# A gated linear attention and MLP-mixer kernel: another hand-fixed issue order and another buffer numbering

## The chip, the cores and the metric

One core of a Trainium2 chip runs the kernel. The metric is the device time of one execution in microseconds, taken as the median of several executions of the same program. The engines of the core work side by side, each through its own queue in order: TensorE (PE, with its weight loads shown apart as PEld), VectorE (DVE), ScalarE (ACT), GpSimd (POOL) and SyncE (SP), whose queue here only issues transfers.

## The reference

The input is q, k, v and alpha of shape (4, 8, 768, 48) and four mixer weights; the output is (4, 768, 384) in float32.

```python
# attention: a recurrence over t, for each of 4 batches and 8 heads
state = alpha[:, :, t, :, None] * state + np.einsum('bhd,bhe->bhde', k[:, :, t], v[:, :, t])
y[:, :, t] = np.einsum('bhd,bhde->bhe', q[:, :, t], state)
# x = y with heads side by side, (4, 768, 384); then the mixer
h = np.maximum(xt @ w_tok1, 0.0) @ w_tok2        # xt is x with tokens last
u = x + h.transpose(0, 2, 1)
out = u + np.maximum(u @ w_ch1, 0.0) @ w_ch2
```

## The kernel before, in words

The recurrence is computed in blocks. Each batch of 768 tokens is cut into 3 blocks of 256, so there are 12 blocks, numbered n = 0 to 11; a block has two halves of 128 tokens, and each SBUF row holds two neighbouring tokens. For block n the kernel loads alpha, k, q and v (`ld_at`, `ld_kt`, `ld_qt`, `ld_vt`, L584, 384 KB each). It takes logarithms on ACT (`ln`, L631, L634, L637), sums them along the tokens on PE (`cum`, `cumw`, L643) and takes exponentials of the sums and of their negatives on ACT (`E`, L676 and L683; `IE`, L679 and L687). k is multiplied by `IE` and q by `E` (`kk`, `qq`, L700, on DVE or POOL). Both products are transposed, on PE for blocks 0 to 5 (`trk`, `trq`, L712, with the evictions `evk`, `evq`, L745 on ACT or L746 on DVE) and by DMA for blocks 6 to 11 (`dk`, `dq`, L725, with one more copy `pq`). `G0_n` and `G1_n` are the products of keys and queries on PE, `mask0_n` and `mask1_n` their masked evictions on DVE (L770). `K` makes the new state, which DVE and POOL add to the old one (`s`, L837; `sa`, L841; `sm`, L844). `ia`, `ib` and `y0`, `y1` give a half's output on PE, and `x0`, `x1` take it out of PSUM.

The mixer of batch b follows. `t1_b_m_kc` (L878) and `t2_b_i` (L883) are the token products with the eviction `ht` between them, and `u_b_i` (L887, DVE) adds x. u is transposed on PE for batch 0 (`up`, L894, with the evictions `ut`) and by DMA for batches 1 to 3 (`ux_b_0` and `ux_b_1`, L729, one for each half of the tokens). `c1_b_mc_half` (L902) is a group of three 384-wide matmuls; `rt_b_mc_half` evicts it with a maximum (L873 on ACT, L875 on DVE). `c2_b_i_q` (L907) is a group of three matmuls over three of the twelve `rt`; `o_b_i` (L911, DVE) adds u and `st_b_i` (L624) stores the result. The weights come in 16 loads of 384 KB (`ldw_wt1`, `ldw_wt2`, `ldw_wc1`, `ldw_wc2`, L600 to L607), each followed by a cast (`cw`). The first six of the twelve column blocks of `wc1` need its pieces 0, 1 and 2, the other six its pieces 3, 4 and 5.

Nothing is scheduled while the program is built. `build` (L121) makes all operations with their inputs and outputs. The table `ORDER` names them one after the other, each with a letter for its engine (t PE, s ACT, v DVE, g POOL, y SP), and they are emitted in exactly that order, so it sets every queue. `BUFS` gives each value its buffer number: 19 buffers for loads (`in`), 8 PSUM banks, 20 for `rt`, 3 for `o`, 2 to 4 for most others. A value waits until the last reader of its buffer is done. `fillers` (L130) offers filler operations named `f8_x`, which multiply zeros into a free PSUM bank ahead of the operation x; the number counts units of one 512-wide matmul, and every three units become one float32 matmul of 64 rows (`fill`, L645). The order lists only some of them. `shared` (L732) makes every SBUF-to-SBUF operation on DVE wait for the last such operation on POOL, and the other way round.

Of the kernel before, what the change touches and what calls it, by code (L numbers as in the profile page):

```python
# [421 lines left out]
rt_0_9_0v rt_0_11_1v E4s c1_0_7_0t c1_0_10_1t c1_0_7_1t ldw_wc10y r14s cw_wc10s rt_0_10_1v trq3t evk3s rt_0_7_0v
ldw_wc12y ld_vt3y cw_wc12g c1_0_2_0t c1_0_0_1t ka3g rt_0_7_1s c1_0_8_1t rt_0_10_0v vb3v vs1_3g vs0_3g rt_0_0_1v
rt_0_2_0v evq3s ld_at5y ld_qt4y c1_0_1_1t rt_0_8_1v c1_0_3_0t kc3s K3t P5g c1_0_4_1t rt_0_3_0s rt_0_1_1s q0r4g G0_3t
ld_kt4y qq4g s0_3v ln15s G1_3t sa1_3v c1_0_2_1t rt_0_2_1s mask0_3v lnP5s c1_0_1_0t c1_0_5_1t rt_0_5_1s rt_0_1_0s r15s
mask1_3v ldw_wc21y cw_wc21s k0a4g ldw_wc20y c1_0_6_1t rt_0_6_1v c1_0_4_0t kk4v ldw_wc22y c1_0_5_0t c1_0_0_0t cw_wc22s
rt_0_4_0v rt_0_0_0v cw_wc20g rt_0_4_1s c1_0_6_0t rt_0_6_0v c1_0_3_1t trq4t rt_0_3_1v cum5t trk4t ld_kt5y k0a5g
ldw_wc23y rt_0_5_0s c2_0_3_0t c2_0_5_0t evq4s kb4s evk4v ld_qt5y G1_4t mask1_4v G0_4t ld_vt4y c2_0_0_0t IE5s c2_0_0_1t
ka4g cw_wc23s c2_0_3_1t kc4s sm1_3g E5s mask0_4v ib3t y1_3t ldw_wc24y cw_wc24s c2_0_5_1t vb4g vs1_4s x1_3s ia4t
ldw_wc25y vs0_4g cw_wc25s ld_at6y y0_3t kk5v c2_0_3_2t y0_4t q0r5v trk5t evk5s qq5v K4t c2_0_0_2t sa0_4v c2_0_0_3t P6v  # L430
x0_3s ld_at7y sm0_4g o_0_0v trq5t x0_4s sa1_4v P7g evq5s lnP6s c2_0_5_2t c2_0_5_3t ld_vt5y vb5g c2_0_4_0t c2_0_4_1t
ld_kt7y kc5g G1_5t G0_5t lnP7s o_0_5v ib4t y1_4t vs1_5s mask1_5v t1_1_1_0t t1_1_1_1t sm1_4g x1_4s c2_0_4_2t c2_0_3_3t
vs0_5s ld_at8y t1_1_1_2t st_0_5s K5t mask0_5v sa0_5v sm0_5v cum6t t1_1_0_0t ld_kt6y k0a6g t1_1_0_1t ld_qt6y c2_0_2_0t
# [532 lines left out]
```

## Time and profile before

| what | us |
|---|---|
| median of three executions | 163.17 (162.33, 163.17, 164.11) |
| span of the profiled execution, first to last instruction | 160.5 |
| what lies around the span, if the profiled execution took the median | 2.7 |
| first instruction to the first `c1` group of batch 0 | 31.76 |
| that point to the end of the last matmul | 125.66 |
| end of the last matmul to the end of the span | 3.08 |

The profiled execution has no time of its own beside its span. The times of the table's lower rows are read off the timeline of PE. A row of a timeline gives the start, the length, the engine, the line and operation, the tiles, the count of merged instructions, and in brackets the engine's idle time ahead of it and what ended that. A matmul's row lasts longer than the distance to the next matmul's start, because matmuls are pipelined: distances between starts say how fast PE works.

### The profile page before, as it was taken

Reading aid. Unit: us, or ns where it says so; the run is one execution under the profiler, and the core shown is the slowest. Engines: PE = TensorE matmul, PEld = TensorE weight load, DVE = VectorE, ACT = ScalarE, POOL = GpSimd, SP = SyncE. Lnnn points to the kernel's source line nnn. Section 1 sums busy time; section 2 is a strip of 40 time slices with the busy share of each in tenths; the row PEclk is TensorE's granted clock in tenths of the full one; section 3 lists DMA queues with packets and bytes.
Section 4 is the critical chain, followed back from the end, with each engine's and each line's share of the span. In section 5 each row is a group of like instructions: output and inputs, shape, how many; then the busy total and the mean of one; then the engine's idle time right before and its main releaser. Section 6 shows DMA issues by size and latency. Waiting matters only on the chain.

```text
span 160.5 us, 3971 instructions
## 1 busy us (share of the span) xinstructions
PE 154.6 (96%) x1563; PEld 97.1 (60%) x1563; DVE 114.9 (72%) x206; ACT 97.8 (61%) x179; POOL 80.8 (50%) x94
## 2 busy tenths in 40 slices
PE   7999989999999999999999999999999999999992
PEld 2545565766667676666667666566567665665661
DVE  6099994979889787989969758795886762464222
ACT  3789999998899955897563583269832203343000
POOL 5205897695973649389778852699523000000000
PEclk9999999999999999999999999999999999999999
DMA  4999999999999999999989999989701235111133
GB/s 122 320 324 317 317 374 311 339 333 306 316 347 324 275 278 272 210 228 319 241 202 298 239 315 204 217 196 134 196 21 62 87 79 169 49 49 53 49 129 116
DMA packets 76130, 35.05 MB, mean 218 GB/s; under 512 B 70352, under 2 KB 74320, under 8 KB 76112
## 3 DMA queue, kind: packets, MB, share of 16 engines
q1 hardware_dynamic: 73808, 31.76, 74.1%
q10 hardware_dynamic: 2304, 3.05, 5.3%
q8 instruction: 12, 0.20, 0.5%
q14 instruction: 6, 0.05, 0.1%
HBM read 25.17 MB, written 4.72 MB: 186 GB/s over the span
## 4 chain that ended last, share of the span: by engine, by line
PE 61%; DMA 12%; DVE 6%; ACT 6%; SPq 6%; POOL 4%; issue 3%; DVEq 0%; POOLq 0%
PE ps L907 22%; PE ps L902 21%; PE ps L643 11%; DMA in<-in_v_dram 6%; SPq L584 6%; DMA out_dram<-o 4%; PE ps L878 3%; PE ps L883 2%; DMA ut<-u 2%; DVE pkk L700 2%; DVE gtm L770 1%; PE ps L712 1%; DVE rt L875 1%; POOL vb L746 1%; POOL pkq L700 1%
## 5 line engine op out<-in xcount | busy, mean ns | idle before, releaser
L907 PE MATMUL ps<-wc,rt 128*128 128x384 bf16 (+1 forms) x300 | 52.4, 319 | 0.0
L902 PE MATMUL ps<-ut,wc 128*128 128x384 bf16 x288 | 50.3, 326 | 0.1
L902 PEld LDWEIGHTS <-wc 128*128 128x128 bf16 x288 | 27.1, 98 | 17.9 <-DMA ut<-u 0.6
L907 PEld LDWEIGHTS <-rt 128*128 128x128 bf16 x300 | 27.8, 98 | 16.0
L873 ACT ACTIVATE rt<-ps 128x384 bf16<-128x384 f32 x47 | 21.4, 492 | 23.6 <-PE ps L902 23.3
L875 DVE TENSOR_SCALAR rt<-ps 128x384 bf16<-128x384 f32 x49 | 25.6, 551 | 9.1 <-PE ps L902 8.9
L770 DVE TENSOR_TENSOR gtm<-ps,mk 128x1024 bf16<-128x1024 f32 x24 | 28.5, 1218 | 3.1 <-PE ps L643 2.8
L911 DVE TENSOR_TENSOR o<-ps,u 128x384 f32<-128x384 f32 (+1 forms) x25 | 13.2, 536 | 12.6 <-PE ps L907 10.1
L700 POOL TENSOR_TENSOR pkk<-in,IE 128x768 bf16<-128x768 f32 x8 | 14.5, 1817 | 3.3 <-DVE ss L844 2.3
L745 ACT CAST x<-ps 128x384 bf16<-128x384 f32 x20 | 9.2, 479 | 11.1 <-PE ps L643 9.5
L887 DVE TENSOR_TENSOR u<-ps,x 128x384 bf16<-128x384 f32 x24 | 12.0, 550 | 3.1 <-PE ps L883 2.5
L746 POOL CAST vb<-in 64x384 bf16<-64x384 f32 (+1 forms) x14 | 8.3, 594 | 10.4 <-DMA in<-in_v_dram 4.7
L692 POOL TENSOR_TENSOR in<-in,in 128x384 f32<-128x384 f32 x8 | 8.0, 1000 | 10.5 <-DVE u L887 3.8
L643 PE MATMUL ps<-rt 128*128 128x512 bf16 (+1 forms) x29 | 12.1, 515 | 1.1 <-DVE rt L541 1.1
L745 ACT CAST vb<-in 64x384 bf16<-64x384 f32 (+1 forms) x18 | 11.4, 634 | 0.8 <-DMA in<-in_v_dram 0.3
L700 POOL TENSOR_TENSOR pkq<-in,E 128x768 bf16<-128x768 f32 x6 | 10.9, 1818 | 0.6 <-DMA tpk<-pkq 0.3
L878 PE MATMUL ps<-x,wt 128*128 128x384 bf16 x48 | 11.0, 325 | 0.0
L844 POOL TENSOR_TENSOR ss<-tmp,E 128x384 bf16<-128x384 f32 x10 | 8.3, 833 | 4.2 <-DVE in L628 3.9
L841 DVE TENSOR_TENSOR tmp<-ps,ss 128x384 f32<-128x384 f32 x16 | 8.8, 552 | 1.8 <-PE ps L643 0.6
L883 PE MATMUL ps<-ht,wt 128*128 128x384 bf16 x48 | 9.1, 326 | 0.0
L643 PE MATMUL ps<-vb,gtm 128*128 128x48 bf16 x192 | 8.2, 183 | 0.2 <-DVE gtm L770 0.2
L643 PE MATMUL ps<-tpq,tpk 48*64 48x128 bf16 (+1 forms) x288 | 7.9, 218 | 0.4 <-POOL tpq L746 0.3
(94 smaller groups left out, 207.6 us busy)
## 6 DMA issues: line engine op xcount, KB each, us to landing
in<-in_alpha_dram SPq DMA_DIRECT2D x12, 384.0 KB, 5.1
in<-in_v_dram SPq DMA_DIRECT2D x12, 384.0 KB, 5.6
in<-in_k_dram SPq DMA_DIRECT2D x12, 384.0 KB, 5.2
in<-in_q_dram SPq DMA_DIRECT2D x12, 384.0 KB, 5.5
in<-in_moe_w_ch_dram SPq DMA_DIRECT2D x12, 384.0 KB, 5.9
out_dram<-o ACTq DMA_DIRECT2D x15, 192.0 KB, 1.8
in<-in_moe_w_tok_dram SPq DMA_DIRECT2D x4, 384.0 KB, 6.0
out_dram<-o SPq DMA_DIRECT2D x8, 192.0 KB, 2.2
```

Of the source, the lines that this page charges most:

```text
L643: return self.pe.matmul(out, lhsT=lhsT, rhs=rhs, start=start, stop=stop, skip_group_check=True)
L700: self.shared(self.eng[e].tensor_tensor(self.t(dst)[:, :, h0:h1, 0:D], self.t(src)[:, h0:h1].rearrange("p h s d -> p s h d"), bass.AP(tens ...
L745: return self.act.copy(d, s)
L770: self.nc.vector.tensor_tensor(self.t(gtm)[:, hf, :, :], self.pair(gp).rearrange("p a (j t) -> p (a j) t", t=128), bass.AP(tensor=m.tensor ...
L873: self.act.activation(d, s, AF.Relu)
L875: self.nc.vector.tensor_scalar_max(d, s, 0.0)
L878: self.pe.matmul(self.bank(bank)[:, 0:HD], lhsT=self.wt1[:, kc, m * 128 : m * 128 + 128], rhs=self.t(x), start=(kc == 0), stop=(kc == NS - 1))
L883: self.pe.matmul(self.bank(bank)[:, 0:HD], lhsT=self.wt2[:, kc, i * 128 : i * 128 + 128], rhs=self.t(hts[kc]), start=(kc == 0), stop=(kc = ...
L887: self.nc.vector.tensor_tensor(self.t(u)[:, i % 3], self.bank(bank)[:, 0:HD], self.t(x), ALU.add)
L902: self.pe.matmul(self.bank(bank)[:, 0:HD], lhsT=self.wc1[:, kc, mc * 128 : mc * 128 + 128], rhs=self.t(ut)[:, 3 * half : 3 * half + 3, kc, ...
L907: self.pe.matmul(self.bank(bank)[:, 0 : cz - ca], lhsT=self.t(rts[mc][0])[:, i * 128 : i * 128 + 128], rhs=self.wc2[:, mc, ca:cz], start=( ...
L911: self.nc.vector.tensor_tensor(self.t(o)[:, ca:cz], self.bank(bank)[:, 0 : cz - ca], self.t(u)[:, i % 3, ca:cz], ALU.add)
```

## The change

The two tables are replaced; no other line differs. The names in the new `ORDER` are the same operations but for the fillers, and what each operation computes is the same. Three things differ: the order on every engine, the engine of 147 operations that may run on more than one, and the buffer numbers. Of the diff, whose rows are tables of names, these lines show the kind:

```diff
-ld_at1y ld_at0y ln1s ln0s f8_cumw1t f1_cumw1t cumw1t IE1s cumw0t IE0s ld_vt0y E0s vb0g vs0_0g vs1_0v ld_kt0y kk0v
+ld_kt1y ld_at0y ln0s f12_cumw0t f2_cumw0t cumw0t ld_at1y ln1s cumw1t ld_qt0y E0s qq0v f2_trq0t trq0t ld_kt0y IE0s kk0v
...
-11 8 0 1 0 0 2 1 2 1 0 12 0 0 0 4 2 1 1 0 4 3 8 1 4 0 0 5 1 6 6 9 0 1 7 0 12 0 0 7 2 0 1 0 0 1 0 1 2 4 1 7 1 3 2 2 1 6
+6 0 0 7 0 0 0 1 1 2 1 1 2 0 7 4 3 0 5 1 7 0 6 1 0 0 0 0 4 8 1 0 4 0 7 2 2 0 5 7 0 1 0 0 10 9 1 6 6 1 4 7 6 0 0 1 1 0 1
```

The fillers before are `f8_cumw1 f1_cumw1 f8_trk0 f1_trk0 f1_trq0 f1_trk1 f2_G0_0 f4_cumw2 f3_y1_0 f2_ia1 f1_G0_2 f1_t1_0_1_5 f3_t2_0_0`, 36 units of which 9 stand ahead of the first `cumw`. Now they are `f12_cumw0 f2_cumw0 f2_trq0 f1_cumw2 f4_trq1 f1_trq1 f4_G1_1 f2_trk2`, 28 units of which 14 stand ahead of the first `cumw`.

The first place is SP's queue at the start of the program, where the loads of blocks 0 to 2 stand. Before, its first nine loads are these (`in_` is a load buffer; the tensor behind the arrow tells alpha, k, q or v):

```order
L584 DMA in_75<-in_alpha_dram 128x8x96
L584 DMA in_72<-in_alpha_dram 128x8x96
L584 DMA in_76<-in_v_dram 128x8x96
L584 DMA in_64<-in_k_dram 128x8x96
L584 DMA in_65<-in_q_dram 128x8x96
L584 DMA in_72<-in_k_dram 128x8x96
L584 DMA in_69<-in_v_dram 128x8x96
L584 DMA in_73<-in_alpha_dram 128x8x96
L584 DMA in_76<-in_q_dram 128x8x96
```

Now they are these:

```order
L584 DMA in_70<-in_k_dram 128x8x96
L584 DMA in_64<-in_alpha_dram 128x8x96
L584 DMA in_65<-in_alpha_dram 128x8x96
L584 DMA in_66<-in_q_dram 128x8x96
L584 DMA in_67<-in_k_dram 128x8x96
L584 DMA in_71<-in_v_dram 128x8x96
L584 DMA in_68<-in_alpha_dram 128x8x96
L584 DMA in_72<-in_v_dram 128x8x96
L584 DMA in_65<-in_q_dram 128x8x96
```

The load of block 1's k now comes first, and q and k of block 0 come ahead of its v. Behind these, the six pieces of `wc1` are loads 20, 21, 22, 24, 25 and 26 before, with a load of q as number 23, and loads 20 to 25 now.

The second place is DVE's queue in the middle of the `c1` groups of batch 0, around the masks of block 3 (`gtm`). Tile numbers are kept: `rt` are evictions of `c1` groups, `vb` a cast of v, `ss` and `tmp` the state, `pkq` the scaled q, `tpq` an eviction of transposed q. Before:

```order
L875 TENSOR_SCALAR rt_3_136<-ps_63 128x384
L875 TENSOR_SCALAR rt_8_141<-ps_63 128x384
L746 CAST vb_0_98<-in_2_66 128x768
L875 TENSOR_SCALAR rt_9_142<-ps_63 128x384
L875 TENSOR_SCALAR rt_6_139<-ps_63 128x384
L875 TENSOR_SCALAR rt_1_134<-ps_63 128x384
L837 TENSOR_TENSOR ss_1_112<-ps_63,E_1_88 128x384
L841 TENSOR_TENSOR tmp_1_110<-ps_63,ss_1_112 128x384
L770 TENSOR_TENSOR gtm_1_108<-ps_63,mk_166 128x1024 x2
```

Now:

```order
L696 TENSOR_TENSOR in_3_67<-in_3_67,lf_0_85 128x8x48
L700 TENSOR_TENSOR pkq_1_93<-in_3_67,E_0_87 128x16x48
L875 TENSOR_SCALAR rt_5_138<-ps_63 128x384
L875 TENSOR_SCALAR rt_0_133<-ps_63 128x384
L746 COPY tpq_1_106<-ps_63 128x2x512
L875 TENSOR_SCALAR rt_8_141<-ps_63 128x384
L875 TENSOR_SCALAR rt_6_139<-ps_63 128x384
L875 TENSOR_SCALAR rt_9_142<-ps_63 128x384
L770 TENSOR_TENSOR gtm_1_108<-ps_63,mk_166 128x1024 x2
L875 TENSOR_SCALAR rt_3_136<-ps_63 128x384
L837 TENSOR_TENSOR ss_1_112<-ps_63,E_0_87 128x384
L841 TENSOR_TENSOR tmp_0_109<-ps_63,ss_1_112 128x384
```

The scaling of block 3's q (`in_3` and `pkq_1`) and the eviction of its transpose (`tpq_1`), which were POOL's and ACT's before, now stand in DVE's queue, and the cast `vb_0` left it. From the first `rt` up to the eviction of `c1_0_10_1`, DVE now has 14 `rt`, two masks, two evictions of transposed q, one of transposed k, the two scalings of q and two of the state.

The third place is SP's queue ahead of the DMA transposes of u for batch 2 (`ut` from `u`). Before:

```order
L584 DMA in_82<-in_k_dram 128x8x96
L584 DMA in_73<-in_q_dram 128x8x96
L584 DMA in_69<-in_v_dram 128x8x96
L584 DMA in_64<-in_k_dram 128x8x96
L624 DMA out_dram<-o_155 128x384
L624 DMA out_dram<-o_153 128x384
L729 DMA_TRANSPOSE ut_131<-u_128 128x9x128
L729 DMA_TRANSPOSE ut_131<-u_127 128x9x128
L725 DMA_TRANSPOSE tpk_103<-pkq_93 128x8x128
L725 DMA_TRANSPOSE tpk_102<-pkk_96 128x8x128
```

Now:

```order
L725 DMA_TRANSPOSE tpk_104<-pkk_96 128x8x128
L725 DMA_TRANSPOSE tpk_103<-pkq_92 128x8x128
L584 DMA in_79<-in_v_dram 128x8x96
L584 DMA in_81<-in_k_dram 128x8x96
L584 DMA in_64<-in_q_dram 128x8x96
L584 DMA in_73<-in_q_dram 128x8x96
L584 DMA in_76<-in_k_dram 128x8x96
L725 DMA_TRANSPOSE tpk_101<-pkq_93 128x8x128
L725 DMA_TRANSPOSE tpk_102<-pkk_94 128x8x128
L729 DMA_TRANSPOSE ut_131<-u_127 128x9x128
L729 DMA_TRANSPOSE ut_131<-u_128 128x9x128
```

The two stores (`out_dram`) ahead of the transposes of u left this queue, the transposes of block 9 (`tpk` from `pkq` and `pkk`) moved ahead of them, and five loads instead of nine stand behind the transposes of block 8. Around the same stage for batch 1, PE now has two `c2` groups, `cum8`, `K6` and five `c1` groups between the end of `t2_1_5` and the first `c1` group of the second half, `c1_1_7_1`.

Of the 25 stores, 15 moved between the queues of ACT and SP. The last three before were issued by ACT (`st_3_4`), ACT (`st_3_1`) and SP (`st_3_0h0`, a half), and now by SP (`st_3_5`), SP (`st_3_1`) and ACT (`st_3_0h1`, a half).

128 lines of the change are left out of this document (64 added, 64 removed), and 20 rows, old and new, of the table BUFS.

## The prediction

> **What bounds the kernel now.** I read the page's head and the chain of waits first, then the busy time by stretches, the timeline of PE from end to end, and the timelines of the other engines around each place where PE's starts are late. All times are us from the span's start.
>
> ```profile
> PE 154.6 (96%) x1563; PEld 97.1 (60%) x1563; DVE 114.9 (72%) x206; ACT 97.8 (61%) x179; POOL 80.8 (50%) x94
> PE 61%; DMA 12%; DVE 6%; ACT 6%; SPq 6%; POOL 4%; issue 3%; DVEq 0%; POOLq 0%
> 0.00:31.76 31.76, 29.45 (x318) 16.62 (x319) 23.30 (x52) 26.39 (x40) 18.40 (x30) 1.00 1.03 302
> 31.76:157.42 125.66, 125.19 (x1246) 80.44 (x1246) 91.20 (x153) 71.46 (x140) 62.38 (x64) 1.00 0.76 200
> 133.81 10.89 PE L902 MATMUL ps<-ut,wc 128*128 128x384 bf16 x66
> 144.54 2.11 PE L907 MATMUL ps<-wc,rt 128*128 128x384 bf16 x12
> ```
>
> PE is the bound, but not in the whole span. The last two rows give its dense rate: 66 matmuls of 384 columns from 133.81 to 144.54, 10.73/66 = 0.1626 us each, so a `c1` or `c2` group of three takes 0.488. From 31.76, the first `c1` group, to 157.42 PE runs almost without a gap. Before 31.76 transfers keep the DMA engines full (share 1.03), PE waits for the other engines, and fillers make up much of its 29.45 us. So the span is three terms: a head of 31.76, 125.66 of PE work with few holes, and a tail of 3.08. A new order can shorten the head, close holes, or open new ones; the work in the middle term is the same.
>
> Five late starts are all the holes over 0.1 us that I find in the middle term:
>
> ```profile
> 45.63 0.17 PE L643 MATMUL ps<-off,idn 128*128 128x16 bf16 x1
> 45.87 0.61 PE L712 MATMUL ps<-idn,pkk 128*128 128x128 bf16 x8
> 46.31 1.14 PE L907 MATMUL ps<-wc,rt 128*128 128x384 bf16 x6
> 47.40 0.62 PE L643 MATMUL ps<-tpq,tpk 48*128 48x128 bf16 x16
> 52.14 1.14 PE L907 MATMUL ps<-wc,rt 128*128 128x384 bf16 x6
> 53.31 0.61 PE L712 MATMUL ps<-idn,pkq 128*128 128x128 bf16 x8
> 100.91 3.82 PE L902 MATMUL ps<-ut,wc 128*128 128x384 bf16 x21
> 104.72 0.64 PE L643 MATMUL ps<-tpq,tpk 48*64 48x128 bf16 x32
> 115.67 0.33 PE L643 MATMUL ps<-ss,tpq 128*128 128x96 bf16 x4
> 116.29 0.64 PE L643 MATMUL ps<-tpq,tpk 48*64 48x128 bf16 x32 [0.28 <-POOL tpq L746]
> ```
>
> Each hole is the distance between two starts less the dense time of what lies between. `trk4`: 45.87 - 45.63 less 0.03 is 0.21. `G1_4`: 1.09 less 6 x 0.1626 is 0.11. `trq5`: 1.17 less 0.98 is 0.19. The first seven `c1` groups of batch 2, at the transposes of u: 3.81 less 21 x 0.1626 is 0.40. `G1_11`: 0.62 less 0.17 is 0.45. In all 1.36.
>
> **The change, the head.** What ends it are loads and a chain through DVE, POOL and PE.
>
> ```profile
> 5.47 0.84 ACT L637 ACTIVATE la<-in 128x768 bf16<-128x768 f32 x1 [0.35 <-DMA in<-in_alpha_dram]
> 6.91 1.39 POOL L746 CAST vb<-in 128x768 bf16<-128x768 f32 x2 [4.11 <-DMA in<-in_v_dram]
> 24.76 0.82 POOL L746 CAST wt<-in 128x768 bf16<-128x768 f32 x1 [0.56 <-DMA in<-in_moe_w_tok_dram]
> 30.16 0.88 POOL L746 CAST wc<-in 128x768 bf16<-128x768 f32 x1 [0.36 <-DMA in<-in_moe_w_ch_dram]
> 6.37 0.65 PE L643 MATMUL ps<-la,u 128*128 128x384 bf16 x3
> 7.45 0.81 ACT L687 ACTIVATE IE<-ps 128x768 f32<-128x768 f32 x1 [0.32 <-PE ps L643]
> 1.06 4.21 PE L643 MATMUL ps<-rt 128*64 128x384 f32 x7 [1.06 <-DVE rt L541]
> 7.34 2.26 PE L643 MATMUL ps<-rt 128*64 128x384 f32 x7
> 21.30 1.30 DVE L746 COPY tpq<-ps 128x1024 bf16<-128x1024 bf16 x1
> 23.17 2.36 DVE L770 TENSOR_TENSOR gtm<-ps,mk 128x1024 bf16<-128x1024 f32 x2
> 28.27 2.88 DVE L887 TENSOR_TENSOR u<-ps,x 128x384 bf16<-128x384 f32 x6 [0.83 <-PE ps L883]
> 16.84 1.82 POOL L700 TENSOR_TENSOR pkk<-in,IE 128x768 bf16<-128x768 f32 x1 [2.30 <-DVE ss L844]
> ```
>
> Loads: number 2 lands by 5.47, 3 by 6.91, 17 by 24.76 and 22 by 30.16, 1.28 each from 3 to 17, and (5.40 - 2 x 1.28)/3 = 0.95 for each of the three weights among the last five. Both orders need 22 loads, and then a cast of 0.88, for the first `c1`: not before 31.04 in either. The new alpha of block 0 is load 2, so its logarithm ends near 6.3. The fillers ahead of its sum are 14 units; the first row of fillers shows 9 units in 4.1 us (0.46 each) and the second 9 in 2.26 (0.25). Nine slow units and five fast ones end near 6.4, so they cost about 0.1 beyond the load, at most 1.1 if all are slow.
>
> From there DVE sets the pace. Its new order up to the last mask of block 2 starts near 8.3, when the exponential of block 0 is done: the sums before began at 6.37, nearly the same time, and ACT had the result at 7.45, plus 0.83. It holds 15.7 us of work at start-to-start distances: six masks at 1.13 (2.36 for two that overlap), one eviction of transposed q at 1.2, three scalings at 0.87, three of transposed k at 0.6, and seven 384-wide ones at 0.47. Its one long wait: `evq1` needs `trq1`, which needs `qq1`, 1.82 on POOL, which needs load 9, near 14.6; that is ready near 17.0, DVE at 16.2, so 0.85, and another 0.8 for waits below 0.2. The last mask ends near 25.7, against 23.17 + 2.36 = 25.53 before. From that mask to the first `u` it was 28.27 - 25.53 = 2.74, through `y1_2`, `x1_2`, the last `t1`, `ht` and the first `t2`, the same work now: six `u` end near 31.2, `ut_0_0` near 31.7. The first `c1` starts near 31.65: the head gives -0.1. Its bounds: -0.7 (the cast of load 22) and +1.1 (load 9 later, or slow fillers).
>
> The pieces 0 to 2 of `wc1` are loads 23 to 25 now; at 0.95 each behind 30.1 the last lands near 33.0 and its cast ends near 33.9; the seventh `c1` group is the first to need them, at 31.65 + 6 x 0.488 = 34.6. Costed at nothing; the cover is 0.7.
>
> **The holes.** For each hole I follow what it waited for.
>
> ```profile
> 93.33 3.16 SPq L624 DMA_DIRECT2D out_dram<-o  x2
> 96.97 3.29 SPq L729 DMA_TRANSPOSE ut<-u  x2
> 64.68 1.29 SPq L729 DMA_TRANSPOSE ut<-u  x1
> ut<-u SPq DMA_TRANSPOSE x6, 3.0
> 31.76:46.31 14.55, 14.48 (x126) 9.37 (x127) 12.68 (x23) 13.06 (x24) 11.26 (x12) 1.00 1.04 324
> 34.88 2.46 DVE L875 TENSOR_SCALAR rt<-ps 128x384 bf16<-128x384 f32 x5 [0.42 <-PE ps L902]
> L875 DVE TENSOR_SCALAR rt<-ps 128x384 bf16<-128x384 f32 x16 | 8.0, 550 | 1.0 <-PE ps L902 1.0
> L700 DVE TENSOR_TENSOR pkk<-in,IE 128x768 bf16<-128x768 f32 x1 | 1.0, 957 | 0.5 <-POOL in L692 0.5
> ```
>
> `trk4` and `trq5` waited for scalings on DVE; now `kk4`, `qq4` and `qq5` follow each other on POOL. From 36.5, when the scaled q of load 26 frees POOL, its queue takes 0.83 + 1.0 + 0.5 + 1.82 to `kk4`, 1.0 + 1.0 + 1.82 more to `qq4`, and three casts, 1.0 and 1.82 to `qq5`: 40.6 where PE needs it at 43.2, 44.4 for 44.9, 49.7 for 51.4. The 0.40 go. The transposes of u for batch 2 stood behind two stores that held SP for 3.16; now the stores are ACT's, and the second transpose can go out near 98.3 and land 3.1 later, 101.4, for a group due near 101.9: the 0.40 go. `G1_11` waited for `pq11` on POOL; it is ACT's now, and its transpose is queued earlier: the 0.45 go. `G1_4` stays a hole, since `evq4` is on DVE and late: 0.1 becomes 0.2.
>
> New holes. Between `t2_1_5` and `c1_1_7_1` stand 7 groups, `cum8` and `K6`, 4.0 us, where `u` (0.55), SP's other transpose and the transpose itself (1.29 to issue each, 3.0 to land) need 4.0 if SP is free and 5.0 if it is not: between 0 and 1.0, and I take 0.3, nearer the free end, because `dq6` ahead of it is ready in time. `K4` needs `vs0_4` at the end of ACT's row of casts: due and ready both near 52.2; 0 to 0.5, taken as 0.1. `c1_3_10_0` is used by a `c2` group only 0.74 later, where one eviction alone takes 0.55 behind the matmul's end: 0.1. For what no order shows I take 0.3, a little above one average hole of before (1.36/5); 0 to 1.36 is its range. Sum of the middle: -0.40 - 0.40 - 0.45 + 0.1 + 0.3 + 0.1 + 0.1 + 0.3 = -0.35.
>
> **The tail.**
>
> ```profile
> 156.45 0.56 DVE L911 TENSOR_TENSOR o<-ps,u 128x384 f32<-128x384 f32 x1 [0.91 <-PE ps L907]
> 157.44 0.36 DVE L911 TENSOR_TENSOR o<-ps,u 128x192 f32<-128x192 f32 x1 [0.43 <-PE ps L907]
> out_dram<-o ACTq DMA_DIRECT2D x3, 192.0 KB, 1.8
> out_dram<-o SPq DMA_DIRECT2D x1, 96.0 KB, 1.6
> ```
>
> A half tile is still last, 1.6 behind its issue. But the whole tile before it is finished only half a tile of PE work (0.5) earlier instead of a whole one (0.98), so its 1.8 ends about when the half's does, and both share the DMA engines: +0.1, bounds 0 and +0.4.
>
> **Sum.** -0.1 - 0.35 + 0.1 = -0.35: a span near 160.15. The median of the runs shown is 2.7 above the profiled span; with the same around it, 163.17 - 0.35 = 162.8.
>
> **A rule of the Trainium skill beside it.** The rows of fillers show the same nine units in 4.1 us first and in 2.26 later, while the granted clock reads 1.00 in both. In "TensorE: Matmul & The Clock Gate", section "What's actually happening", the array starts at half clock, doubles after some 3.4 us of activity in a free-running window, and falls back after an idle window as long. The trace agrees with the first part; no run here shows the second. By the rule, the longest gap that I work out for PE in the new head (under 1 us) is no danger, and the sum stays; a rival takes the other case.
>
> **Rivals.** Within 1%, 161.5 to 164.8, is about what a measurement of this kernel can tell from no change.
>
> A, the sum above: 162.8, chance 0.42.
>
> B, nothing gained: each hole only moves, because every order fills PE the same and waits for whatever comes last. For it: the counts of work on all engines are nearly the same. Against it: two of the holes have named causes that are gone. 163.2, chance 0.14.
>
> C, faster: the head at its bound (-0.7), all holes closed (-1.36), no new ones, tail +0.1: 163.17 - 1.96 = 161.2, chance 0.18. For it: margins of 0.5 to 2.6 above. Against: five holes stayed in an order just as tight.
>
> D, slower: DVE becomes the bound in the `c1` groups of batch 0. From the first `rt` to that of `c1_0_10_1` it has 14 `rt` at 0.48 (the row of five, less one length, over four), two masks at 1.13, two `evq` at 1.2, and 0.6, 0.87, 0.47 and 0.94 for `evk3`, `qq3`, `q0r3` and the state: 14.2 us, where PE's work from the first `c1` to the end of `c1_0_10_1` is 14.9. Its first `rt` cannot start before the second group ends, near 32.8, so it ends at 47.0 without one wait. Before it was busy 12.68 of 14.55 and waited 1.5 (1.0 and 0.5 in the rows above). With that again it ends at 48.5, 2.0 behind PE's place there (46.5), and the masks of block 4 come next on DVE, so nothing makes it good: 162.8 + 2.0 and 0.2 in `K4`, 165.0. It decides once the eviction of `c1_0_10_1` ends after 47.5. I give it 0.20: 8 banks hide about half a us of lag, and the waits need not come again.
>
> E, slower: with 14 units of filler behind the first `cumw` instead of 27, the array falls to half clock in the head. Some ten PE steps of the chain, 0.3 to 0.6 each, then double: +3, 165.8. Chance 0.06; every gap there is under 1 us, and 1.06 us of idling before the first filler is all that the trace shows ahead of slow rows.
>
> **The numbers.** Forecast 162.8, the likeliest case's time. Faster by over 1%: C, 0.18. Within 1%: A and B, 0.56. Slower: D and E, 0.26. The range reaches down to C at 161.2 and up to D, 165.0; beyond it are E and the outer parts of C and D, under 0.2.
>
> **What would show it.** Right: the first `c1` of batch 0 starts between 31.1 and 32.5; `trk4`, `trq5` and `G1_11` start without a hole; POOL, not DVE, is where `trk4`'s key comes from; the first `c1` groups of batch 2 run at 0.488 each; PE's gaps behind the first `c1` sum to 1 us or less. Wrong: a first `c1` after 33, a hole over 0.5 at the transposes of batch 1, DVE busy above 95% from 32 to 47 with PE waiting for `rt`, or fillers and sums at twice their times behind 8 us.

## The result, and the profile after

| | median | executions | ratio to before, 95% interval |
|---|---|---|---|
| before | 162.90 | 20 | |
| after | 165.12 | 20 | 1.0108 (1.008 to 1.0135) |
| after, in two other sets of runs | 164.20 and 165.29 | 12 and 6 | 1.0068 (1.0028 to 1.0107), 1.0128 (1.0071 to 1.0185) |

The change makes the kernel about 1% slower; 162.8 was forecast. The ratios leave out executions over 1.5% above the fastest of their kernel, seven of the twenty after and one of the twenty before, and the medians hold them, so the medians lie 1.4% apart. The times also spread more: 163.0 to 168.1 after, against 161.9 to 164.1 and a single 166.8 before. Every execution's time is 1.7 above its span (164.51 and 162.8 for the profiled one), so the profiled execution of before, with 160.5, took 162.2: it was a quick one, and what lies around the span is 1.7, not the 2.7 that I took from the median.

The stretches up to the first `c1` group and from there to the last matmul, in the profile after:

```profile
0.00:32.30 32.30, 28.34 (x310) 16.39 (x311) 23.31 (x52) 24.90 (x38) 20.66 (x31) 1.00 1.01 301
32.30:159.46 127.16, 125.65 (x1248) 80.36 (x1246) 92.41 (x154) 72.19 (x140) 58.59 (x63) 1.00 0.77 196
```

Against 31.76, 125.66 and a tail of 3.08, the head is 0.54 longer, the middle 1.50 and the tail (162.8 - 159.46 = 3.34) 0.26.

PE's rows in the profile after where block 4's k (`trk4`, 44.05), its q (45.68) and block 5's q (`trq5`, 52.32) are transposed, where the `c1` groups of batch 2 begin, and at the first matmuls of block 11 (`G1_11`, 116.18):

```profile
44.05 0.61 PE L712 MATMUL ps<-idn,pkk 128*128 128x128 bf16 x8
45.68 0.61 PE L712 MATMUL ps<-idn,pkq 128*128 128x128 bf16 x8
52.32 0.61 PE L712 MATMUL ps<-idn,pkq 128*128 128x128 bf16 x8
...
104.26 5.05 PE L902 MATMUL ps<-ut,wc 128*128 128x384 bf16 x30
109.15 0.33 PE L643 MATMUL ps<-vb,pkk 128*128 128x96 bf16 x4
...
115.91 0.34 PE L643 MATMUL ps<-ss,tpq 128*128 128x96 bf16 x4
116.18 0.64 PE L643 MATMUL ps<-tpq,tpk 48*64 48x128 bf16 x32
```

No row has a wait in brackets. The 30 matmuls at 104.26 take 4.89 to the next row, 0.163 each, so the hole at u's transposes of batch 2 is gone, and `G1_11` comes 0.27 behind the row ahead of it where it came 0.62 behind before. All that was to close did close, 1.25 in all, and the three small holes that I expected at `G1_4`, `K4` and `c1_3_10_0` did not come. But these rows of PE, from 68 to 92, show what opened:

```profile
68.11 0.17 PE L643 MATMUL ps<-off,idn 128*128 128x16 bf16 x1
68.69 0.34 PE L643 MATMUL ps<-vb,pkk 128*128 128x96 bf16 x4 [0.42 <-DVE pkk L746]
68.87 0.33 PE L643 MATMUL ps<-vb,kt 128*128 128x96 bf16 x4
69.41 2.60 PE L902 MATMUL ps<-ut,wc 128*128 128x384 bf16 x15 [0.20 <-DMA ut<-u]
72.27 5.54 PE L902 MATMUL ps<-ut,wc 128*128 128x384 bf16 x33 [0.26 <-DMA ut<-u]
...
85.71 0.65 PE L902 MATMUL ps<-ut,wc 128*128 128x384 bf16 x3
86.83 0.33 PE L643 MATMUL ps<-vb,pkk 128*128 128x96 bf16 x4 [0.47 <-POOL vb L746]
...
91.17 0.36 PE L643 MATMUL ps<-vb,gtm 128*128 128x48 bf16 x8
91.66 0.32 PE L643 MATMUL ps<-la,u 128*128 128x384 bf16 x1
```

By starts less dense time the holes are 0.55 at `K6` (68.69), 0.37 and 0.42 at the first `c1` groups of the two halves of batch 1, 0.63 at `K7` (86.83) and 0.29 at `cum9` (91.66). With 0.19 at `K5` they make 2.45, where I had 0.8 for new holes.

These are SP's rows ahead of the first three of these holes, and POOL's and DVE's ahead of `K7` and `cum9`:

```profile
64.04 1.96 SPq L725 DMA_TRANSPOSE tpk<-pkk  x1
66.10 1.30 SPq L729 DMA_TRANSPOSE ut<-u  x1
67.51 1.25 SPq L725 DMA_TRANSPOSE tpk<-pkq  x1
68.89 1.42 SPq L729 DMA_TRANSPOSE ut<-u  x1
```

```profile
83.21 0.82 POOL L746 CAST vb<-in 128x768 bf16<-128x768 f32 x1 [1.91 <-DMA in<-in_v_dram]
84.43 1.00 POOL L628 TENSOR_TENSOR in<-in 128x384 f32<-128x384 f32 x1 [0.39 <-DMA in<-in_alpha_dram]
85.38 0.84 POOL L844 TENSOR_TENSOR ss<-tmp,E 128x384 bf16<-128x384 f32 x1
86.28 0.50 POOL L746 CAST vb<-in 64x384 bf16<-64x384 f32 x1
```

```profile
91.05 0.56 DVE L911 TENSOR_TENSOR o<-ps,u 128x384 f32<-128x384 f32 x1 [0.94 <-DMA out_dram<-o]
```

Here PE uses a transpose of u 3.3 behind its issue (66.10 to 69.41, 68.89 to 72.27), and the second of u goes out only when SP has issued that of block 6's q. `sm1_6` and `vs0_7`, which `K7` needs and which were ready long before, stand on POOL behind a cast and a product that wait for loads. And `cum9` needs the PSUM bank that `o_1_5` reads; `o_1_5` waits for a buffer whose store, `st_0_4`, was issued at 87.43 on ACT for a tile that was ready at 69.22. Its landing frees the buffer only 3.6 later, at 91.05. All five end on a transfer.

### The profile page after: what moved, and what is told of

It reads as the page before. It is cut to its first block, busy times and chain, and to the rows that moved or that the text cites. A ratio compares the mean times of both kernels' runs of the same rounds, so it can differ in the third digit from the quotient of the medians.

```text
span 162.8 us, 3954 instructions
## 1 busy us (share of the span) xinstructions
PE 154.0 (95%) x1556; PEld 96.8 (59%) x1556; DVE 116.2 (71%) x207; ACT 97.1 (60%) x178; POOL 79.3 (49%) x94
## 4 chain that ended last, share of the span: by engine, by line
PE 69%; DMA 10%; POOL 8%; DVE 4%; ACT 3%; issue 3%; SPq 0%; POOLq 0%; DVEq 0%
PE ps L907 24%; PE ps L902 22%; PE ps L643 14%; PE ps L878 4%; DMA in<-in_q_dram 3%; PE ps L883 3%; DMA in<-in_v_dram 2%; POOL pkk L700 2%; POOL pkq L700 2%; DMA out_dram<-o 2%; PE ps L712 2%; DMA tpk<-pkk 2%; POOL in L692 1%; DVE gtm L770 1%; DVE u L887 1%
## 5 line engine op out<-in xcount | busy, mean ns | idle before, releaser
L902 PE MATMUL ps<-ut,wc 128*128 128x384 bf16 x288 | 50.9, 326 | 0.5 <-DMA ut<-u 0.5
L873 ACT ACTIVATE rt<-ps 128x384 bf16<-128x384 f32 x51 | 23.0, 489 | 26.3 <-PE ps L902 25.1
L875 DVE TENSOR_SCALAR rt<-ps 128x384 bf16<-128x384 f32 x45 | 23.1, 550 | 14.6 <-PE ps L902 14.6
L844 POOL TENSOR_TENSOR ss<-tmp,E 128x384 bf16<-128x384 f32 x12 | 10.0, 836 | 13.1 <-DVE tmp L841 9.3
L700 POOL TENSOR_TENSOR pkq<-in,E 128x768 bf16<-128x768 f32 x8 | 14.5, 1820 | 2.1 <-ACT E L676 0.8
L643 PE MATMUL ps<-rt 128*64 128x384 f32 (+1 forms) x22 | 10.3, 588 | 1.1 <-DVE rt L541 1.1
L700 POOL TENSOR_TENSOR pkk<-in,IE 128x768 bf16<-128x768 f32 x6 | 10.9, 1817 | 0.3
L745 ACT CAST x<-ps 128x384 bf16<-128x384 f32 x13 | 6.2, 478 | 6.5 <-PE ps L643 6.5
L745 ACT COPY tpq<-tpk 128x1024 bf16<-128x1024 bf16 x6 | 8.1, 1353 | 3.2 <-DMA tpk<-pkq 3.2
L628 POOL TENSOR_TENSOR in<-in 128x384 f32<-128x384 f32 x9 | 9.0, 999 | 1.7 <-DVE pkk L700 1.1
```

Source lines behind the costliest of these rows:

```text
L643: return self.pe.matmul(out, lhsT=lhsT, rhs=rhs, start=start, stop=stop, skip_group_check=True)
L700: self.shared(self.eng[e].tensor_tensor(self.t(dst)[:, :, h0:h1, 0:D], self.t(src)[:, h0:h1].rearrange("p h s d -> p s h d"), bass.AP(tens ...
L745: return self.act.copy(d, s)
L873: self.act.activation(d, s, AF.Relu)
L875: self.nc.vector.tensor_scalar_max(d, s, 0.0)
L902: self.pe.matmul(self.bank(bank)[:, 0:HD], lhsT=self.wc1[:, kc, mc * 128 : mc * 128 + 128], rhs=self.t(ut)[:, 3 * half : 3 * half + 3, kc, ...
```

## The experiments

Theory: these places are the loss, each waits for one transfer, and each can be closed. Rival: holes only move, since transfers end each stretch at their own time. For the head the theory was at first the longer filler. A ratio stands for time against the kernel before, with its 95% interval.

**The filler, and three other edits.**

```diff
-ld_kt1y ld_at0y ln0s f12_cumw0t f2_cumw0t cumw0t
+ld_kt1y ld_at0y ln0s f8_cumw0t f1_cumw0t cumw0t
```

> The changed kernel with 9 units of filler ahead of the first sum instead of 14 (the old kernel's number); nothing else is different. Theory (the places that the changed profile shows): all 14 units ran slow, 0.43 each, and the sum began at 7.01 where its logarithm was ready near 6.3, so with 9 units it begins near 6.3 and the first c1 group comes 0.5 to 0.7 earlier, 31.6 to 31.8 instead of 32.30; the time falls by 0.5, to about 164.6. Rival 1 (loads end the head, whatever the start): the first c1 stays within 0.2 of 32.30 and the time within 0.2 of 165.1. Rival 2 (the array needs the longer burst to reach its full rate): the fillers of 9 units and the first sums are slow for longer, first c1 at 32.3 or later.

1.0134 (1.0074 to 1.0193), first `c1` at 32.38. The sum began at 6.42 as expected, and nothing was gained. Rival 2 came in part: the second sum ran at about half its rate (its first three matmuls in 1.12 instead of 0.65), so this profile does not clear the filler alone; a later kernel with all 14 units and an early first `c1` does. The slow sums are taken up at the end.

In the second kernel `ux_1_0y ux_1_1y dk6y ... dq6y` stand in this order on SP, and `kc6s`, `K6t` behind.

> The changed kernel with both transposes of u of batch 1 ahead of those of block 6's k and q on SP, and K6, which waits for the transpose of k, twelve c1 groups later (its copy kc6 on ACT, the copies of k for block 7 behind it on POOL). Theory: the three holes from 68.2 to 72.3 (0.55, 0.37, 0.42) come from SP's row alone; the first c1 of batch 1 starts near 68.4 instead of 69.41, c1_1_7_1 follows without a hole over 0.1, and the time falls by 0.9 to 1.3, to about 164.0. Rival 1 (every order fills PE the same, a closed hole opens again further on): the first c1 of batch 1 comes earlier, but the first t1 group of batch 2 less than 0.4 earlier, time within 0.4 of 165.1. Rival 2 (the u's on DVE, late behind kk6, set the transposes, not SP's row): the first c1 not before 69.2, time within 0.2.

1.0329 (1.0274 to 1.0385). A miss: 1.60 at `c1_1_5_1`, which I had given a PSUM bank of `K6`'s pair, 1.31 at the first `c1` of batch 1, whose transpose took 4.0 to land, 2.03 at `cum9`, and a first `c1` at 33.88. My edit cost more than the holes that it was to close.

```diff
-rt_1_10_1s vb8g
+rt_1_10_1s sm1_6g vs0_7g vb8g
...
-rt_1_2_0s s0_6v
+rt_1_2_0s st_0_4s s0_6v
```

> The changed kernel with sm1_6 and vs0_7 ahead of the cast vb8 on POOL instead of behind P9, which waits for a load, and the store of o_0_4 issued twenty us earlier on ACT. Theory: K7's hole (0.63) shrinks to under 0.15 and that of cum9 (0.29) closes: the time falls by 0.6 to 0.9, to about 164.4. Rival 1 (holes move): K7 and cum9 start without their holes, but the first c1 of batch 2 less than 0.3 earlier, time within 0.3 of 165.1. Rival 2 (K7 waits next for the copy of k for block 7 on ACT, which ends at 86.02): K7's hole falls by 0.2 at most.

1.0051 (1.001 to 1.0092): 0.9 less than by the change's first ratio, as the theory has it, though the intervals overlap. `K7`'s hole is 0.14, `cum9`'s nothing; `K8` waited 0.90 for the transpose of block 8's k.

> The three edits of the other kernels of this set together. Theory: their gains add: 0.5 + 1.1 + 0.75 = 2.3 less, about 162.8, equal to the old kernel or below it; the head, c1 of batch 1 and K7 each as in the kernels that have one edit alone. Rival (holes move, or the loss is spread over many small delays): the sum falls short by half or more, 164.0 or above.

1.0191 (1.0144 to 1.0237): 1.60 at `c1_1_5_1` as in the second kernel, 1.85 at `c1_1_7_1` and 1.39 at `t1_1_1_5` outweigh the rest.

**Repeats, and one edit at a time.** The change as it is:

> The changed kernel as it is, for a second profile of it. In the runs so far the sum of block 9 (cum9) waited 0.29, 2.11 and 2.03 for the buffer of o_1_5, in three kernels that leave that place as the change has it, and not at all in the two that send the store of o_0_4 early. Theory (the loss hangs on how long transfers take in an execution): c1 groups, G's and all of PE behind 98 as before, but the waits on transfers from 58 to 97 (K6, the first c1 of batch 1, c1_1_7_1, K7, cum9) differ by 0.3 to 2 from the first profile; cum9's is 0.3 to 2.1. Time 164.7 to 165.5. Rival (the holes are set by the order alone, and the two of 2 us come from my edits): the same holes within 0.2 each, cum9 0.3.

1.0068. The wait on DVE for the store's buffer, and `cum9` behind it:

```profile
91.39 0.56 DVE L911 TENSOR_TENSOR o<-ps,u 128x384 f32<-128x384 f32 x1 [2.42 <-DMA out_dram<-o]
...
92.00 0.32 PE L643 MATMUL ps<-la,u 128*128 128x384 bf16 x1 [1.68 <-DVE o L911]
```

1.83 where the first profile had 0.29, while `K6` waited 0.05 (0.55) and `K7` 0.20 (0.63). The theory's first half holds: one order, other holes.

> The changed kernel with the store of o_0_4 on ACT behind the copy of block 6's q instead of behind a logarithm of block 9; nothing else is moved. Theory: cum9 starts without a hole, the time falls by the mean of the holes seen (0.29, 2.11, 2.03), so by 0.8 to 1.8, about 163.8. Rival 1 (K7's wait on POOL carries the gain of the kernel that had both edits): 0.3 at most, 164.8. Rival 2 (holes move): cum9 closes and K8 or G0_8 waits as long; time within 0.3 of 165.1.

1.0037 (0.9999 to 1.0074), on the same chip 0.5 below the change by ratio: short of the 0.8 that was the least expected, and within the intervals. Over all profiles the place is plain: nine were taken with the store late, and `cum9` waited 0.29, 0.49, 0.69, 1.12, 1.19, 1.58, 1.83, 2.03 and 2.11; nine with the store early, and it never waited. That only 0.5 was won of a mean of 1.26 suggests that something near it ends next, though the interval is too wide to show it; in this profile `c1_1_7_1` waited 1.53 for its transpose instead of 0.42.

```diff
-ld_at2y ld_vt1y ld_qt1y
+ld_at2y ld_qt1y ld_vt1y
```

> The changed kernel with block 1's q loaded ahead of block 1's v, one load earlier. The kernel with 9 units of filler had its first sum at 6.42 instead of 7.01 and yet the first c1 at 32.38: the fillers don't set the head. Theory: qq1 on POOL, which waits 0.49 for that load, and behind it evq1 on DVE, which waits 0.57, set it: qq1 starts at 14.5 instead of 14.96, the last mask of block 2 ends near 25.7 instead of 26.16 and the first c1 starts near 31.85 instead of 32.30; the time falls by 0.45, to about 164.7. Rival (DVE and POOL make it good or lose it behind: POOL's row of three scalings, the loads of the weights): the first c1 within 0.15 of 32.3.

The first `c1` came at 31.65, with all 14 units of filler in place, but the time did not fall: 1.0123 (1.0068 to 1.0177). So few executions cannot show 0.45.

> The changed kernel with u's transposes of batch 1 each one place earlier on SP (ahead of block 6's k and of its q), block 6's scaled k on POOL instead of DVE, kc6 on ACT and K6 five c1 groups later. The earlier try put both transposes ahead and K6 twelve groups later; it lost 3.4, of which 1.6 came at c1_1_5_1, whose PSUM bank I had given it straight behind K6's, and 1.0 at the first c1, with weights that landed late. Theory (SP's row and kk6 on DVE make the holes): the first c1 of batch 1 starts at once behind cum8, near 68.4 instead of 69.41, no hole over 0.2 up to c1_1_5_1; the time falls by 0.7 to 1.2, about 164.2. Rival 1 (the transposes land 4 us behind their issue whatever the order, since loads for block 7 are in front of them): first c1 at 69.2 or later, no gain. Rival 2 (K6 waits as long in its new place): K6 with a hole over 0.4.

1.0199 (1.0143 to 1.0255). The first `c1` of batch 1 followed `cum8` at once and `c1_1_7_1` waited 0.11, so SP's row does make these holes. But `cum8` was itself 0.71 late, since block 6's scaled k, now on POOL, stood ahead of block 8's product, `c1_1_3_1` waited 0.64 and `K7` 0.86.

**Before once more, and edits together.**

> The kernel before as it is, for a second profile of it: the first was of an execution 0.7 below the median. Theory (the old order waits on transfers less, in every execution): first c1 between 31.5 and 32.1, no hole over 0.5 behind it, holes in all 1.2 to 2. Rival (the first profile was a lucky one, the old order has holes of 1 to 2 on transfers too): at least one hole over 0.8, holes in all over 2.5.

0.9991 (0.9944 to 1.0038). POOL's copy of block 11's q, and PE's first matmuls of that block:

```profile
116.59 1.32 POOL L746 COPY tpq<-tpk 128x1024 bf16<-128x1024 bf16 x1 [2.33 <-DMA tpk<-pkq]
...
117.97 0.64 PE L643 MATMUL ps<-tpq,tpk 48*64 48x128 bf16 x32 [1.55 <-POOL tpq L746]
```

The rival was right here: the hole at `G1_11` is 1.72 in this execution and was 0.44 in the first; the middle takes 127.54 (31.54 to 159.08) instead of 125.66. The old order has its own wait on a transfer, and its first profile was of an execution in which that was short. The head is short in both: 31.76 and 31.54.

```diff
-ld_vt8y ... ld_at9y ... ld_qt9y ... ld_at10y ... dk8y ... dq8y
+ld_vt8y ... dk8y ... ld_at9y ... ld_qt9y ... ld_at10y ... dq8y
...
-st_3_1y ... st_3_0h1s
+st_3_1s ... st_3_0h1y
```

> The changed kernel with five edits that leave PE's, DVE's and nearly all of ACT's row alone: the store of o_0_4 early; sm1_6 and vs0_7 ahead of vb8; the transpose of block 8's k ahead of three loads; block 1's q loaded ahead of its v; the last two stores on the other's queue. Theory: cum9 (0.3 to 2.1), K7 (0 to 0.64) and K8 (0 to 0.9) without holes, first c1 near 31.8, tail 3.1 instead of 3.34: against the change as it is (165.1 and 164.2 in two sets) 1.5 less, near 163.1, as the kernel before; what is left over it is the wait for u's transposes, 0.6 to 1. Rival 1 (holes move): the holes close, others of as much in all open behind them, and the time stays above 164. Rival 2 (the changed kernel's other stretches are faster, 1.25 of closed holes): under 162.5.

1.0094 (1.0056 to 1.0132): nothing gained; rival 1. `cum9` and `K8` start without a hole at 90.60 and 89.69, but PE's next row is:

```profile
92.44 0.64 PE L643 MATMUL ps<-tpq,tpk 48*64 48x128 bf16 x32 [0.91 <-ACT tpq L745]
```

`G0_8` waited 1.07 for the transpose of block 8's q, behind three loads. A second wait of almost the same end stood behind the first. The first `c1` was at 32.56, where the weights' casts ended late, and the tail 3.38: the queue of the last two stores is not what makes it longer.

> The changed kernel with u's transposes of batch 1 one place earlier on SP as in the last try, but block 6's scaled k left on DVE (on POOL it had put off cum8 by 0.71 and K7 by 0.86) and the eviction of c1_1_3_0 on ACT ahead of the copy of block 6's q (0.64 at c1_1_3_1). Theory: first c1 of batch 1 straight behind cum8 and c1_1_7_1 without a hole: 0.7 to 1.0 less than the change, 164.1 against 164.9 for the mean of its two sets. Rival 1 (transposes land 4 or more behind their issue in most executions): a hole of 0.4 or more at c1_1_8_0 or c1_1_7_1. Rival 2: K6 or a group behind it waits as long as was won.

1.0211 (1.0144 to 1.0278), a miss: the first `c1` of batch 1 waited 1.11 for its transpose (rival 1), `K7` 0.85 and `c1_1_0_1` 1.35.

> The edits of the two kernels above together. Theory: the gains add, 162.3, at or below the kernel before; PE from the first c1 to its end in 126 or less. Rival (holes move): no better than the one with five edits.

1.0122 (1.0054 to 1.0189), 1.37 at `c1_1_0_1` again. In both that group waits for the eviction of `c1_1_5_1`, whose PSUM bank it takes, as in the change itself; on ACT that eviction stands behind copies of block 8's v, and those behind the load of that v, for which POOL's cast waited 2.91 here and 1.91 in the change. I found no way of moving `K6` that won.

**What stands behind the first wait.** The change as it is, as the base on one chip:

> The changed kernel as it is, once more, on the same chip as the next three, as their base; a third profile. In seven kernels that leave SP's row between 76 and 98 alone, the G0 of block 8 started between 92.35 and 93.14, whatever was won or lost before it. Expected: 92.3 to 93.2 again, cum9's hole 0.2 to 2.1, first c1 32.0 to 32.5, time 164.2 to 165.2.

1.0128. `G0_8` came at 94.52, so its constant start was chance. The first `c1` in this execution, and POOL ahead of it:

```profile
33.81 1.47 PE L902 MATMUL ps<-ut,wc 128*128 128x384 bf16 x8 [1.57 <-POOL wc L746]
...
32.90 0.85 POOL L746 CAST wc<-in 128x768 bf16<-128x768 f32 x1 [1.74 <-DMA in<-in_moe_w_ch_dram]
```

The next one has the edits of the third kernel, and on SP and POOL:

```diff
-ld_at9y ... P9g ... ld_qt9y ... ld_at10y ... dk8y kc8g ... dq8y
+dk8y dq8y ld_at9y ... kc8g P9g ... ld_qt9y ... ld_at10y
```

> The changed kernel with the store of o_0_4 early, sm1_6 and vs0_7 ahead of vb8 on POOL, and now both transposes of block 8 ahead of the loads of blocks 9 and 10 on SP (before, three loads stood ahead of them; the kernel with five edits moved that of k alone, and G0_8 then waited 1.07 for that of q), kc8 ahead of P9 on POOL. Theory (behind cum9's wait stands a second one of nearly the same end, the transpose of block 8's q behind three loads): now G0_8 starts near 91.4 where the base has 92.3 to 93.2, and the time is 0.9 to 1.3 below the base. Rival (a third wait behind it, say for P9, whose load comes later now): G0_8 within 0.3 of the base, the hole at cum9 or K8 instead, no gain.

1.0064 (1.002 to 1.0108), 1.05 below the base by ratio, as expected, though the two intervals overlap. `cum9` and `K8` have no hole, `G0_8` 0.14; `ib7` waited 0.47. But `G0_8` started at 94.70, no earlier than the base's 94.52 and far from 91.4: this profile is of a long execution (166.65), with 0.96 lost at `trq4`, 0.61 at `K6` and 1.12 at `c1_1_7_1` ahead of it. So the gain rests on the times and is not read off this profile.

For the head, with block 1's q ahead of its v as above:

```diff
-evq2s cw_wt10s
+cw_wt10s evq2s
```

> The changed kernel with block 1's q loaded ahead of its v, and the cast of wt1's first piece on ACT ahead of the copy of block 2's q. In the profiles of the change the load of block 4's alpha stands 1.3 on SP until that cast frees its buffer, and the weights behind it land late: wc1's casts end at 31.7 to 32.1. Theory (two bounds end the head, the chain through qq1 and these loads): with both moved the first c1 starts near 31.4 to 31.6, 0.6 to 0.8 before the base, and the time falls by as much. With q's load alone it was 31.65 in one profile and the time did not fall; rival 1: the waits behind take it back, time within 0.3 of the base. Rival 2 (bandwidth alone sets the loads): the first c1 within 0.25 of the base.

1.0082 (1.0035 to 1.0128), 0.75 below the base by ratio, not resolved; by the median, 165.89 against 165.29, nothing is gained. The first `c1` was at 32.98 in its profile, straight behind the cast of the last weight, which waited 1.43 for its load: the cast's new place did not bring the weights early in this execution.

> The edits of the two kernels above together. Theory: both gains, 1.5 to 2 below the base: 162.8 to 163.3, as fast as the kernel before, with the waits for u's transposes (0.6 to 1) left in it. Rival (holes move, transfers end each stretch at their own time): less than 0.8 below the base.

1.0071 (1.0032 to 1.0111): 0.93 below the base, no more than one of the two; the gains did not add. First `c1` at 31.73. A new hole has a plain cause, on POOL, DVE and PE:

```profile
86.77 0.99 POOL L628 TENSOR_TENSOR in<-in 128x384 f32<-128x384 f32 x1 [2.87 <-DMA in<-in_alpha_dram]
...
87.79 0.56 DVE L844 TENSOR_TENSOR ss<-tmp,E 128x384 bf16<-128x384 f32 x1 [1.41 <-POOL in L628]
...
89.07 0.33 PE L643 MATMUL ps<-ss,tpq 128*128 128x96 bf16 x4 [0.62 <-DVE tmp L841]
```

The load of block 9's alpha, which I had put back, holds `P9`, and because the kernel makes DVE and POOL take turns on such operations, DVE waits for `P9`, and PE for DVE.

So that load goes ahead again, and `kc8` behind `P9`:

```diff
-dk8y dq8y ld_at9y ... kc8g P9g
+ld_at9y dk8y dq8y ... P9g kc8g
```

> The changed kernel with the edits of the last double one, except that the transposes of block 8 stand behind the load of block 9's alpha: in that kernel P9 waited for this load to 86.77, and the shared port's order held sm0_7 on DVE, and ib7 on PE (0.79), behind P9. Theory (every hole has its transfer in front of it, and can be closed): no hole over 0.4 from K7 to G0_8; the time 0.3 to 0.7 below the 164.5 of the double one, near 163.9. Rival (the gains don't add, since transfers end each stretch at their own time): 164.3 or more, and a hole over 0.5 between 76 and 98 in another place.

1.0011 (0.9973 to 1.005), a median of 163.40 against 162.98. PE from `K7` to the masks of block 8:

```profile
86.41 0.65 PE L902 MATMUL ps<-ut,wc 128*128 128x384 bf16 x3
86.89 0.33 PE L643 MATMUL ps<-vb,pkk 128*128 128x96 bf16 x4
...
91.24 0.36 PE L643 MATMUL ps<-vb,gtm 128*128 128x48 bf16 x8
91.44 0.32 PE L643 MATMUL ps<-la,u 128*128 128x384 bf16 x1
...
92.31 0.64 PE L643 MATMUL ps<-tpq,tpk 48*64 48x128 bf16 x32
```

No wait is left from 73 to 92 but the 0.09 that every `G` has, and the first `c1` starts at 31.49. So the theory holds for this stretch: each hole had a transfer ahead of it, and they close when all of them are moved. The 1% is gone; against before there is no difference that can be measured. Two limits stand beside it. The change as it is was not run in this set, so it is compared with its ratios of the other sets. And this profile shows only part of the gain: `K6` waited 0.69 and `c1_1_7_1` 1.30 ahead of the dense stretch, so the middle takes 127.69 (31.49 to 159.18), no less than in the change (127.16, 127.60 and 127.76 in its three profiles); only the head is shorter.

> The kernel above, with the second transpose of u of batch 1 ahead of that of block 6's q on SP, the copy of that q later on ACT, and the eviction of c1_1_3_0 ahead of it. Theory: c1_1_7_1, which waited 0.23 to 0.5 in most profiles and 1.1 to 1.5 in three, starts at once; 0.3 to 0.6 less than the kernel above, 163.3 to 163.6, within 0.3% of the kernel before. Rival: the copy of q, now later, makes G1_6 or the evictions late, and nothing is won.

1.0103 (1.005 to 1.0156). `c1_1_7_1` starts without a hole, and the rival is right:

```profile
76.11 2.11 PE L902 MATMUL ps<-ut,wc 128*128 128x384 bf16 x12 [0.49 <-ACT rt L873]
```

The later copy of q holds ACT's evictions; in this execution the weights were late too (first `c1` at 32.96). No version beat the kernel before.

## Why the prediction was wrong

- **The time around the span.** 2.7 was 1.7. With 1.7 my span of 160.15 is a forecast of 161.85: this error hid 1.0 of the others. The median after is 3.3 above that, of which 0.7 is that the profiled execution of before was a quick one.
- **The holes that close**: right, one by one, and for the reasons given; 1.25 of the 1.36 went. But they were sized on one execution: `G1_11`, taken at 0.45, was 1.72 in the other.
- **The holes that open**: the step that failed, as a term of the sum. "Between 0 and 1.0, and I take 0.3, nearer the free end" for the transposes of u was 0.79, and 0.55 at `K6` belongs to the same row of SP. "For what no order shows I take 0.3 ... 0 to 1.36 is its range" was 0.29 + 0.63 in the first profile, and 0.49 to 2.11 at `cum9` alone in the other eight that leave the store late. Both could be read ahead of the result: the order shows `st_0_4` nine names ahead of `o_1_5`, which takes its buffer, and `sm1_6` and `vs0_7` behind two operations that wait for loads. A late store alone is no sign: in the kernel before, the same store stood 24 us behind its tile (69.64 and 93.33) and nothing waited for it, since no operation took that buffer so soon behind it. I followed the waits that the profile before showed, and not the buffers and queues that the new order makes tight.
- **The head**: -0.1 forecast, +0.54, +0.44 and +2.05 (33.81) in the change's three profiles against the first of before. Two bounds took turns. In the first profile it was the chain that I named, through load 9, `qq1` and `evq1`, with its wait too small in my sum: `evq1` started at 17.49, not 17.0, since load 9 held `qq1` to 14.96. That half us stayed to the end. These are DVE's `evq1`, its last mask and its first `u`, and PE's last transposes of u and first `c1` groups:

```profile
17.49 1.32 DVE L746 COPY tpq<-ps 128x1024 bf16<-128x1024 bf16 x1 [0.57 <-PE ps L712]
...
24.93 1.22 DVE L770 TENSOR_TENSOR gtm<-ps,mk 128x1024 bf16<-128x1024 f32 x1
...
28.81 2.88 DVE L887 TENSOR_TENSOR u<-ps,x 128x384 bf16<-128x384 f32 x6 [0.74 <-PE ps L883]
```

```profile
31.90 0.50 PE L894 MATMUL ps<-idn,u 128*128 128x128 bf16 x6
32.30 5.53 PE L902 MATMUL ps<-ut,wc 128*128 128x384 bf16 x33
```

The mask ends at 26.15, where I had 25.7; the first `u` is 0.54 behind its 28.27 of before, all that the head lost; and PE goes on to the first `c1` without a wait. The other bound is the loads of the weights, which I had ending where they did before. In the second profile `evq1` came at 16.89, and the last weight's cast ended at 32.13, right ahead of the first `c1`; in the third PE waited 1.57 for that cast. Both orders need 22 loads, but the new one gets the last of them later. These rows of the first profile are ACT's cast of the first piece of wt1 (with the next one), SP's load of block 4's alpha, and POOL's cast of the last weight, which ended at 31.69 where it ended at 31.04 before:

```profile
21.05 1.55 ACT L745 CAST wt<-in 128x768 bf16<-128x768 f32 x2
...
21.89 1.63 SPq L584 DMA_DIRECT2D in<-in_alpha_dram  x1
...
30.81 0.88 POOL L746 CAST wc<-in 128x768 bf16<-128x768 f32 x1
```

That load follows the one ahead of it by 1.30 (19.88 + 0.70 = 20.58 to 21.89), at the end of the cast that frees its buffer, and from 15 to 25 the transfers move 315 GB/s (the last column; after, and then before) where before they moved 341:

```profile
15.00:25.00 10.00, 8.93 (x120) 5.27 (x119) 9.23 (x14) 9.21 (x16) 9.33 (x8) 1.00 1.06 315
```

```profile
15.00:25.00 10.00, 9.14 (x160) 6.40 (x159) 9.69 (x12) 9.24 (x16) 7.41 (x8) 1.00 1.12 341
```

With block 1's q loaded early, `evq1` came at 16.54 and the first `c1` at 31.65: so much for the chain. With the cast moved too, the first `c1` came at 31.73 and 31.49 in two profiles and at 32.98 and 32.96 in two others, right behind the last weight's cast. So the cast's place does not decide by itself when the weights land, and the cause of that stays open.
- **The tail**: +0.1 forecast, +0.26 measured, inside its bounds.
- **Rivals**: B was the nearest in mechanism for the middle (127.16, 127.60 and 127.76 against 125.66 and 127.54): one wait on a transfer, at `G1_11`, was exchanged for another, at `cum9`. D's 165.0 is the nearest number, by luck. Its lag came: the eviction of `c1_0_10_1` ended at 48.62, behind the 47.5 that D named. Its cost did not: DVE was busy 13.22 of 14.97 up to the last of these `c1` groups, 88%, and PE all of it, and PE had no hole over 0.1 from there to 58.

```profile
32.30:47.27 14.97, 14.97 (x148) 9.88 (x147) 13.22 (x22) 12.65 (x26) 11.84 (x13) 1.00 1.08 323
```

What is shown: the holes that opened end on the transfers named, since each closed in at least one kernel that moved its transfer or what stood behind it, and `cum9` in nine profiles of nine; and with the late store, POOL's queue, block 8's transposes and the head's load and cast all moved, the 1% is gone. What stays open: how the 1% divides among them, since single edits moved the time by less than their intervals; where the kernel without the 1% won its time in the middle, since its one profile shows as long a middle as the change's; and the waits of batch 1 (`K6`, `c1_1_7_1`), which no try closed without opening others.

## What to carry to other kernels

Where a new order closes holes that a profile shows, look in it for what the profile cannot show: for each buffer class with few buffers, how far the release (a store, a cast) stands ahead of the operation that takes the buffer next, and for each queue, what stands behind an operation that waits for a load. One profile gives one draw of the transfers' times: a hole of 0.45 on a transfer was 1.72 the next time, so size such holes from several. Behind a wait on a transfer a second of nearly the same end stood here twice, so close all of a stretch before you judge one.

## What the runs showed of the hardware

A wait of 2 us at `cum9` cost more than its length in both profiles that have one. In the profile with 9 units of filler, these are PE's two first sums, and the stretch behind `cum9`'s wait of 2.11:

```profile
6.42 0.65 PE L643 MATMUL ps<-la,u 128*128 128x384 bf16 x3 [1.64 <-ACT la L637]
...
7.66 1.12 PE L643 MATMUL ps<-la,u 128*128 128x384 bf16 x3 [0.20 <-ACT la L637]
```

```profile
92.10:96.80 4.70, 4.62 (x54) 2.62 (x54) 3.77 (x6) 3.32 (x7) 2.58 (x2) 0.64 0.94 291
```

The granted clock (the last column but two) falls to 0.64 on average over 4.7, and nine `c2` matmuls took 2.52 (94.14 to 96.66) instead of 1.46. The same came behind the 2.03 of the second kernel; waits of 1.83 and 1.85 in other profiles left the rate full. "TensorE: Matmul & The Clock Gate", section "What's actually happening", of the Trainium skill gives an idle window of about 3.4 before the array falls back; here 1.64 and 0.20 of idling in the head, and 2.03 and 2.11 later, were enough. So what my rival E describes exists: in the head of this kernel with 9 units, and in the middle of two of the twenty profiles. With the change's own 14 units no profile shows it in the head. The mean granted clock of every execution is on record: it is 0.99 or less in 12 of 170 executions of the change and its variants, these two profiled ones among them, and in none of the kernel before in the same sets; ten of the 12 are of kernels that leave the store of `o_0_4` late.
